# A two-branch attention kernel: its units ordered by a table of places, q and k in column halves, weight loads in halves on two queues, and warm-up matmuls on zeros

## The chip, the cores and the metric

The kernel runs on one core of one Trainium2 chip. A core has five engines with a queue each: PE (TensorE, matmuls; its weight loads are listed apart as PEld), ACT (ScalarE), DVE (VectorE), POOL (GpSimd) and SP (SyncE, which here only issues DMAs). They run side by side and wait for each other by semaphores. The metric is the device time of one execution in microseconds (us); less is better.

## The reference, cut to what matters

```python
def _A_ref(x, wqkv, w_phi, wo):                 # linear attention, H=32 heads of 20, S=2048, D=640
    q, k, v = ...                               # x @ wqkv, split into heads
    pq, pk = q @ w_phi, k @ w_phi               # per head
    phi_q = concat([softmax(pq), softmax(-pq)]) # phi_k likewise
    kv  = einsum('bhsf,bhsd->bhfd', phi_k, v)
    num = einsum('bhqf,bhfd->bhqd', phi_q, kv)
    den = einsum('bhqf,bhf->bhq', phi_q, phi_k.sum(s)) + 1e-06
    return (num / den) @ wo

def _B_ref(x, wq, wk, wv, wo, beta):            # 4 segments of 512 rows, memory M, z
    for s in range(4):
        a_dot = softmax(qs @ ks.T * scale + causal mask) @ vs
        a_mem = (phi(qs) @ M) / (phi(qs) @ z + 1e-06)   # phi(t) = t+1 if t>0 else exp(t)
        o_s = g * a_mem + (1 - g) * a_dot               # g = sigmoid(beta)
        M += phi(ks).T @ vs; z += phi(ks).sum()
    return concat(o_s) @ wo

g = sigmoid((x * gate_w).sum(-1))
out = g * _A_ref(x, ...) + (1 - g) * _B_ref(x, ...)
```

## The kernel before, in words

x has 2048 rows, worked on as 16 chunks of 128 rows, four chunks to a segment. It is needed with its columns on the partitions (xT): the first four chunks come in plainly (x_nat) and are transposed by PE (L435), the other twelve by transposing DMAs on SP (L363).

Branch B (local attention and memory), per segment: for each chunk the projections to k and q (b_kq, L518, through proj, L506: five matmuls of 128x320 per half of the columns, L510), a copy of each half out of its PSUM bank to kq (L462 on ACT or L464 on DVE), a store of kq to a DRAM buffer kd (L529), and the exponential and min/max of phi(k) (L536, L540, L543). When all four chunks are stored, transposing DMAs bring back groups of four heads as kqT (L864). Per pair of groups, five products of q and k go to the four PSUM banks called st (L893, four row tiles of 32 at once), each is read by one exponential over 2048 columns on ACT into one of six PT buffers (L899), POOL masks the diagonal (L905), and PE multiplies by v (L920, "pv"). There are 80 such products, 20 per segment, and one st, so a product waits until the exponential before it has read st. The memory term is L959 (am) with the update L986 (upd).

Branch A: projections of v and k (a1, L598; k's with folded weights), two exponentials (L609), sums, a reciprocal, a normalisation on POOL (L623), and the products kv (L644, L660). Then, per segment, the products pq (L735) with two exponentials (L743), den (L757), num (L796, read by DVE's ts, L802), and the final projections fin (L843), copied out and stored by chunk (L853).

All products but st share four PSUM banks w_76 to w_79. A bank is held from a group's first matmul until ACT or DVE has read it.

The order of the instructions on every engine is made by a Planner when the kernel is built. Each op has an engine (or two to choose from), an estimated duration, dependences, and a key. The planner walks a modelled time; when an engine is free it takes the ready op with the smallest key (after a flag, pri, that puts ops on a held bank first). Keys come from formulas whose numbers stand in PRM (L26), such as PRM["a0"] + PRM["a1"] * n for the n-th attention step (ak, L858). The engines then run these fixed orders; what waits blocks all behind it on its engine or its DMA queue. Two loads that matter at the start are beta_b (L352) and Wc (L350), small ones on SP; the large weights WkB, WqB, WvB, WvA and WqA are issued whole by ACT.

## Time and profile before

| | |
|---|---|
| median of 3 runs | 338.96 us (337.43 to 340.62) |
| profiled execution, its own time | 342.3 us |
| its span, first to last instruction | 340.6 us |
| PE busy | 306.5 us (90%) |
| ACT busy | 252.9 us (74%) |
| DVE busy | 231.4 us (68%) |
| POOL busy | 203.0 us (60%) |
| mean granted TensorE clock | 0.960 |

The profile is of one execution. Busy time of PE is modelled at the ends of matmuls, so a busy PE may still be slow, and the granted clock is a column of its own: 1.00 is 2.4 GHz, 0.50 is 1.2 GHz. A wait is put down to the engine whose work came last. Idle time matters on the engine that bounds the stretch.

### The profile page before, as it was taken

What the parts mean: (1) busy time and instruction counts of PE and PEld (TensorE: products, weight loads), DVE (VectorE), ACT (ScalarE), POOL (GpSimd) and SP (SyncE); (2) the same over time, 40 slices, a digit from 0 to 9 for tenths busy, and PEclk for the clock granted to TensorE, in tenths of its full rate; (3) what the DMA queues carried; (4) which work ended last, traced back from release to release, by engine and by line L of the source; (5) the groups of instructions that cost most, each with busy time, mean ns of one, the idle gap of its engine ahead of it and who ended that gap; (6) DMA issues with size and microseconds to landing.
All of it is one profiled execution on the core that took longest, in us unless ns stands there. A gap on an engine that the chain in (4) does not pass through costs nothing.

```text
span 340.6 us, 9847 instructions
## 1 busy us (share of the span) xinstructions
PE 306.5 (90%) x4002; PEld 211.0 (62%) x4002; DVE 231.4 (68%) x568; ACT 252.9 (74%) x330; POOL 203.0 (60%) x338
## 2 busy tenths in 40 slices
PE   2699988999899989989999898998999989968996
PEld 2377667666577765667655654665664755645774
DVE  3342686579867789999964877788773887596400
ACT  1367995788785799778899797985699788846342
POOL 8200197748557579497754486667764687588210
PEclk9999995899999999999899997999999999985999
DMA  7845936761012613022787383544488535312421
GB/s 266 295 187 129 137 70 73 159 139 64 2 64 79 163 26 113 14 92 36 251 153 118 141 149 75 142 62 138 101 155 185 96 96 129 80 22 66 120 67 58
DMA packets 78535, 38.42 MB, mean 113 GB/s; under 512 B 65818, under 2 KB 76442, under 8 KB 78490
## 3 DMA queue, kind: packets, MB, share of 16 engines
q1 hardware_dynamic: 75210, 33.70, 42.5%
q10 hardware_dynamic: 3280, 4.10, 3.4%
q8 instruction: 31, 0.51, 0.7%
q14 instruction: 14, 0.11, 0.1%
HBM read 6.42 MB, written 15.60 MB: 65 GB/s over the span
## 4 chain that ended last, share of the span: by engine, by line
PE 49%; DVE 20%; ACT 12%; POOL 9%; issue 5%; DMA 3%; SPq 0%; DVEq 0%; ACTq 0%
PE w_79 L510 6%; PE w_78 L510 6%; PE w_76 L510 5%; PE w_77 L510 5%; PE st_75 L893 4%; DMA beta_b<-in_B_beta_dram 3%; PE w_78 L843 3%; PE w_77 L843 3%; PE w_76 L920 3%; PE w_79 L843 2%; DVE ts_2711 L802 2%; PE w_76 L843 2%; ACT PT_122 L899 2%; ACT PT_121 L899 2%; DVE rm_127 L939 1%
## 5 line engine op out<-in xcount | busy, mean ns | idle before, releaser
L510 PEld LDWEIGHTS <-xT 128*128 128x128 bf16 x800 | 76.3, 100 | 46.3 <-issue 17.1
L899 ACT ACTIVATE PT_118<-st_75 128x2048 bf16<-128x2048 f32 x14 | 26.3, 1877 | 3.5 <-PE st_75 L893 3.5
L899 ACT ACTIVATE PT_117<-st_75 128x2048 bf16<-128x2048 f32 x14 | 26.4, 1883 | 2.9 <-PE st_75 L893 1.9
L899 ACT ACTIVATE PT_121<-st_75 128x2048 bf16<-128x2048 f32 x13 | 24.5, 1882 | 5.1 <-PE st_75 L893 5.0
L899 ACT ACTIVATE PT_122<-st_75 128x2048 bf16<-128x2048 f32 x13 | 24.5, 1882 | 5.0 <-PE st_75 L893 5.0
L899 ACT ACTIVATE PT_120<-st_75 128x2048 bf16<-128x2048 f32 x13 | 24.7, 1899 | 3.1 <-PE st_75 L893 3.1
L899 ACT ACTIVATE PT_119<-st_75 128x2048 bf16<-128x2048 f32 x13 | 24.6, 1895 | 3.1 <-PE st_75 L893 3.0
L905 POOL TENSOR_SCALAR_AFFINE_SELECT PT_117<-PT_117 128x512 bf16<-128x512 bf16 x22 | 14.2, 654 | 10.4 <-ACT PT_117 L899 10.4
L905 POOL TENSOR_SCALAR_AFFINE_SELECT PT_118<-PT_118 128x512 bf16<-128x512 bf16 x23 | 14.8, 656 | 7.1 <-ACT PT_118 L899 7.1
L905 POOL TENSOR_SCALAR_AFFINE_SELECT PT_122<-PT_122 128x512 bf16<-128x512 bf16 x21 | 13.4, 650 | 8.6 <-ACT PT_122 L899 8.6
L905 POOL TENSOR_SCALAR_AFFINE_SELECT PT_119<-PT_119 128x512 bf16<-128x512 bf16 x21 | 13.3, 644 | 6.7 <-ACT PT_119 L899 6.7
L905 POOL TENSOR_SCALAR_AFFINE_SELECT PT_120<-PT_120 128x512 bf16<-128x512 bf16 x20 | 12.9, 651 | 7.3 <-ACT PT_120 L899 7.3
L617 DVE TENSOR_REDUCE ksum_168<-Ek_160 128x32 f32<-128x640 bf16 x16 | 12.6, 813 | 6.4 <-ACT Ek_160 L609 6.4
L735 PEld LDWEIGHTS <-WqA 128*128 128x128 bf16 x100 | 9.4, 99 | 10.9 <-issue 2.5
L920 PEld LDWEIGHTS <-PT_118 128*128 128x128 bf16 x224 | 15.1, 96 | 1.7 <-issue 1.6
L905 POOL TENSOR_SCALAR_AFFINE_SELECT PT_121<-PT_121 128x512 bf16<-128x512 bf16 x21 | 13.7, 665 | 3.2 <-ACT PT_121 L899 3.1
L920 PEld LDWEIGHTS <-PT_117 128*128 128x128 bf16 x224 | 15.1, 96 | 0.5 <-issue 0.4
L617 DVE TENSOR_REDUCE ksum_169<-Ek_161 128x32 f32<-128x640 bf16 x16 | 12.5, 814 | 4.2 <-ACT Ek_161 L609 4.1
L920 PEld LDWEIGHTS <-PT_122 128*128 128x128 bf16 x208 | 14.1, 96 | 1.3 <-issue 1.2
L578 POOL TENSOR_TENSOR Cd_139<-omgS,omg_b 128x128 f32<-128x128 f32 x2 | 0.8, 399 | 22.6 <-DVE omgS L572 22.4
L920 PEld LDWEIGHTS <-PT_121 128*128 128x128 bf16 x208 | 13.7, 96 | 0.8 <-issue 0.4
L920 PEld LDWEIGHTS <-PT_119 128*128 128x128 bf16 x208 | 14.1, 97 | 0.1
(658 smaller groups left out, 1100.0 us busy)
## 6 DMA issues: line engine op xcount, KB each, us to landing
kd_60<-kq_95 SPq DMA_DIRECT2D x2, 512.0 KB, 2.6
kd_61<-kq_96 SPq DMA_DIRECT2D x2, 512.0 KB, 3.3
kd_62<-kq_97 SPq DMA_DIRECT2D x2, 512.0 KB, 2.8
kd_63<-kq_95 SPq DMA_DIRECT2D x2, 512.0 KB, 3.4
out_dram<-osb_2724 SPq DMA_DIRECT2D x6, 160.0 KB, 1.9
WkB<-in_B_wk_dram ACTq DMA_DIRECT2D x1, 800.0 KB, 5.3
WqB<-in_B_wq_dram ACTq DMA_DIRECT2D x1, 800.0 KB, 8.1
WvB<-in_B_wv_dram ACTq DMA_DIRECT2D x1, 800.0 KB, 11.5
```

The lines of the kernel that those rows point to most:

```text
L510: nc.tensor.matmul(w[:, 0:width], lhsT=T["xT"][:, c, sc * P:(sc + 1) * P], rhs=T[Wn][:, c, 320 * hf:320 * hf + width], start=(c == 0), sto ...
L578: nc.gpsimd.tensor_tensor(out=T[dst][s % 2], in0=og[:, :, None].to_broadcast([P, 4, H]), in1=T[src][:, None, :].to_broadcast([P, 4, H]), o ...
L617: op("DVE", 0.74, lambda sgn=sgn: nc.vector.tensor_reduce(out=T["ksum"][js][:, H * sgn:H * sgn + H], in_=T["Ek"][ik][:, sgn].rearrange("p ...
L735: nc.tensor.matmul(w, lhsT=T["WqA"][:, c, t * P:(t + 1) * P], rhs=T["xT"][:, c, s * L:(s + 1) * L], start=(c == 0), stop=(c == KC - 1))
L802: op("DVE", dve_t(320), lambda w, sgn=sgn: nc.vector.tensor_tensor(out=T["ts"][d][:, sgn], in0=w[:, 0:320].rearrange("p (h d) -> p h d", d ...
L843: nc.tensor.matmul(w[:, 0:320], lhsT=T[nm][j][:, k5, :], rhs=T[Wo][:, k5, hf * 320:hf * 320 + 320], start=(i == 0), stop=(i == 9))
L893: nc.tensor.matmul(st4[:, i, o:o + w], lhsT=T["kqT"][j][r:r + 32, 0, c * P:(c + 1) * P], rhs=T["kqT"][j][r:r + 32, 1, c * P:L], start=True ...
L899: op("ACT", act_t(2048), lambda: nc.scalar.activation(out=T["PT"][slot], in_=st4, func=ACT.Exp, scale=SCALE_B), r=("st4",), w=(("PT", slot ...
L905: nc.gpsimd.affine_select(out=v, in_=v, pattern=[[0, 4], [1, P]], compare_op=ALU.is_ge, fill=0.0, base=0, channel_multiplier=-1)
L920: nc.tensor.matmul(w[:, j * 84 + i * V1:j * 84 + (i + 1) * V1], lhsT=T["PT"][slot][:, i, o + (j - c) * P:o + (j - c + 1) * P], rhs=T["vB"] ...
L939: nc.vector.tensor_tensor(out=rd, in0=rd, in1=T[C][s % 2][:, :, 4 * g:4 * g + 4], op=ALU.mult)
```

## The change

**Order.** PRM goes. A table of 441 numbers gives a key to each unit of work: one projection with its copy, one step of attention, one group of kv, and so on. The keys of ops in one unit are equal. The formulas stay only as defaults. The planner's estimates change too (shorter hops to the next engine, shorter pv and st products, one DMA line for both queues with at most eight transfers under way), ops that only later members of a bank's group need are made to hold back the group's first op, and non-attention groups no longer need two free banks to begin.

**q and k in halves.** b_kq works on one half of the columns of one chunk: two projections, two copies, a store of 128x1024, phi(k) of 320 columns. kq is half as wide and has six buffers. Transposes of heads of one half wait only for the four stores of that half. phik's halves and the exponentials' buffers are kept apart.

**Loads.** WkB, WqB and WvB come in halves of 320 columns, some on ACT's queue and some on SP's. WvA and WqA move to SP, behind the first stores. sig_b's exponential gets a later key.

**Start.** DVE zeroes a tile, ACT runs one exponential on it, PE runs NWARM = 12 matmuls of 128x512 on it. All four copies of xT are DVE's.

**End.** The output of a chunk is stored in two halves.

```diff
-PRM = {"a0": -9.65, "a1": 0.97, "v0": 2.4, "v1": 2.28, "i1": 3.91, "d1": 3.58, "i2": 24.29,
...
+TABLE = (32379, -8395, -7202, -45515, -9326, -21479, -14085, -40063, -5810, 810, -5549, -11546,
...
-    HOP = {"PE": 0.27, "ACT": 0.20, "DVE": 0.18, "POOL": 0.13, "SP": 0.1, "X": 0.0}
+    HOP = {"PE": 0.20, "ACT": 0.18, "DVE": 0.18, "POOL": 0.12, "SP": 0.1, "X": 0.0}
...
+    def unit(self, default):
+
+        n = len(self.keys)
+        self.keys.append(self.table[n] / 100 if n < len(self.table) else default)
+        return Unit(n)
...
+        for lst in banks.values():
+            head, busy = lst[0], sum(o.dur[0] for o in lst if "PE" in o.eng)
+            for o in lst[1:]:
+                for p in o.preds:
+                    if p.bank is not head.bank and p not in head.preds:
+                        head.preds[p] = 0.0 if "PE" in o.eng else busy
...
-                        need = 1 if o.att else 2
-                        if n < need:
+                        if not n:
                             continue
-                        st = max(st, sorted(free)[need - 1])
+                        st = max(st, min(free))
+                    if o.q is not None:
+                        st = max(st, lands[0])
...
-    dma(wload("WkB", B_wk, q="ACT"), (), ("WkB",), -1998, 819, eng="ACT")
-    dma(wload("WqB", B_wq, q="ACT"), (), ("WqB",), -1997, 819, eng="ACT")
...
+    xload(0)
+    wpart("WkB", B_wk, 0, -1998)
+    xload(2)
+    wpart("WqB", B_wq, 0, -1997)
+    wpart("WkB", B_wk, 1, -1996, eng="SP")
+    wpart("WqB", B_wq, 1, -1995)
+    wpart("WvB", B_wv, 0, -1994, "WvBw", eng="SP")
+    wpart("WvB", B_wv, 1, -1993, "WvBw")
...
+    dma(wload("WvA", A_wqkv[:, 2 * D:3 * D]), (), ("WvA",), -10, 819, release=15.0)
+    dma(wload("WqA", A_wqkv[:, D:2 * D]), (), ("WqA",), -9, 819, release=18.0)
...
+    op("DVE", 0.13, lambda: nc.vector.memset(T["PT"][0][:, 0], 0.0), w=(("PT", 0),), key=-4000)
...
+    op("ACT", 1.4, lambda: nc.scalar.activation(out=T["rd"][0][:, 0], in_=T["PT"][0][:, 0, 0:4],
+                                                func=ACT.Exp), r=(("PT", 0),), w=(("rd", 0),), key=-1996.5)
+    for i in range(NWARM):
+        op("PE", 0.43 if i < 8 else 0.22, lambda: nc.tensor.matmul(
+            st4[:, 0, :], lhsT=T["PT"][0][:, 0, 0:P], rhs=T["PT"][0][:, 0, :], start=True,
+            stop=True), r=(("PT", 0),), w=("st4",), key=1e6)
...
-        op(("DVE", "ACT"), (0.7, 0.6), cp, w=(("xT", sc),), free=bk)
+        op("DVE", 0.42, lambda w, cp=cp: cp("DVE", w), w=(("xT", sc),), free=bk, key=-1000)
...
-    def b_kq(s, c, key):
-        i = (4 * s + c) % NKQ
+    def b_kq(s, c, hf, key):
+
+        i = (8 * s + 4 * hf + c) % NKQ
...
-            hv + (("kq", i),), (("kd", s, c),), key, 524)
+            (("kq", i, 0), ("kq", i, 1), ("kq", i)), (("kd", s, c, hf),), key, 262)
...
-                                                     scale=-1.0), r=("beta_b",), w=("sig",))
+                                                     scale=-1.0), r=("beta_b",), w=("sig",), key=-15)
...
-        ch = 4 * s + qc
-        dma(lambda: nc.sync.dma_start(out=out2[ch * P:(ch + 1) * P, :], in_=T["osb"][n]),
-            (("osb", n, 0), ("osb", n, 1)), (("out", ch),), key, 164)
+            rows = slice((4 * s + qc) * P, (4 * s + qc + 1) * P)
+            dma(lambda hf=hf, rows=rows: nc.sync.dma_start(
+                out=out2[rows, hf * 320:hf * 320 + 320],
+                in_=T["osb"][n][:, hf * 320:hf * 320 + 320]),
+                (("osb", n, hf),), (("out", s, qc, hf),), key, 82)
...
-            tuple(("kd", s, c) for c in range(4)), (("kqT", j),), key, 262, tr=True)
+            tuple(("kd", s, c, g // 4) for c in range(4)), (("kqT", j),), key, 262, tr=True)
```

The order itself at three places. First the beginning of DVE's row before the change: xT are the copies of the transposed chunks, WphiD needs Wc and sig_b needs beta_b.

```order
L377 CAST ident_b<-ident_f 128x128
L446 COPY xT<-w_77 128x5x128
L421 TENSOR_TENSOR WphiD<-Wc,m_92 128x140
L404 CAST ind<-bd_93 128x4
...
L421 TENSOR_TENSOR WphiD<-Wc,m_92 128x160
L446 COPY xT<-w_79 128x5x128
L454 COPY WvB<-w_76 128x5
...
L589 TENSOR_SCALAR sig_b<-sig_b 128x32
```

And the same place of the changed kernel, to the first gate column of WvB.

```order
L447 MEMSET PT_121 128x256
L448 CAST ident_b<-ident_f 128x128
L481 CAST ind<-bd_93 128x4
L523 COPY xT<-w_76 128x5x128
L523 COPY xT<-w_77 128x5x128
L617 TENSOR_SCALAR phik_101<-kq_95 128x16x20
L541 CAST kq_96<-w_79 128x4x4x20
L620 TENSOR_TENSOR phik_101<-phik_101,ek_107 128x16x20
L523 COPY xT<-w_76 128x5x128
L523 COPY xT<-w_77 128x5x128
L531 COPY WvB<-w_77 128x5
```

Four copies of xT instead of two stand on DVE, and all of them ahead of the first WphiD; the other two were ACT's, one of them behind sig_b.

Second, the end of the start on SP, before the change: kd are the stores of q and k, kqT the transposes that need all of the segment's stores.

```order
L348 DMA gw_row<-in_gate_w_dram 5x128
L350 DMA Wc<-in_A_w_phi_dram 128x5x20
L352 DMA beta_b<-in_B_beta_dram 128x32
L529 DMA kd_60<-kq_95 128x2048
L529 DMA kd_60<-kq_96 128x2048
L529 DMA kd_60<-kq_97 128x2048
...
L864 DMA_TRANSPOSE kqT_108<-kd_60 128x2x512
L363 DMA_TRANSPOSE xT<-in_A_x_dram 128x5x128
L864 DMA_TRANSPOSE kqT_109<-kd_60 128x2x512
```

And now:

```order
L396 DMA WkB<-in_B_wk_dram 128x5x320
L396 DMA WvB<-in_B_wv_dram 128x5x320
L419 DMA gw_row<-in_gate_w_dram 5x128
L421 DMA Wc<-in_A_w_phi_dram 128x5x20
L425 DMA beta_b<-in_B_beta_dram 128x32
L606 DMA kd_60<-kq_95 128x1024
L606 DMA kd_60<-kq_98 128x1024
L396 DMA WvA<-in_A_wqkv_dram 128x5x640
L606 DMA kd_60<-kq_97 128x1024
L606 DMA kd_60<-kq_96 128x1024
L396 DMA WqA<-in_A_wqkv_dram 128x5x640
L950 DMA_TRANSPOSE kqT_112<-kd_60 128x2x512
```

Two weight halves stand among the first loads, the four stores ahead of the first transpose are half as wide, and the two large weights of branch A stand between them.

Third, the end of ACT's row before the change, at the last eight of the 80 exponentials (PT); dz and osb are copies out of w banks.

```order
L899 ACTIVATE PT_117<-st_75 128x2048
L899 ACTIVATE PT_118<-st_75 128x2048
L462 COPY dz_2703<-w_76 128x128
L899 ACTIVATE PT_119<-st_75 128x2048
L899 ACTIVATE PT_120<-st_75 128x2048
L899 ACTIVATE PT_121<-st_75 128x2048
L899 ACTIVATE PT_122<-st_75 128x2048
...
L462 CAST osb_2724<-w_78 128x320
```

And now, from the 74th to the 78th:

```order
L985 ACTIVATE PT_122<-st_75 128x2048
L824 ACTIVATE Eq_3407<-w_79 128x512 x2
L985 ACTIVATE PT_123<-st_75 128x2048
L539 CAST osb_3437<-w_76 128x320
L985 ACTIVATE PT_124<-st_75 128x2048
L539 COPY dz_3413<-w_76 128x128
L985 ACTIVATE PT_125<-st_75 128x2048
L539 COPY dz_3414<-w_78 128x128
L985 ACTIVATE PT_126<-st_75 128x2048
L539 CAST osb_3436<-w_77 128x320
```

Exponentials that stood back to back now have another operation of ACT between them.

## Rows read from the trace of the kernel before

**Rows 1.** The page: the span, and busy time of each engine.
```profile
span 340.6 us, 9847 instructions
PE 306.5 (90%) x4002; PEld 211.0 (62%) x4002; DVE 231.4 (68%) x568; ACT 252.9 (74%) x330; POOL 203.0 (60%) x338
```
**Rows 2.** Stretches: us, busy PE, PEld, DVE, ACT, POOL; granted clock, DMA share, GB/s.
```profile
0.00:17.30 17.30, 8.05 (x41) 5.04 (x42) 5.41 (x14) 3.96 (x7) 9.20 (x33) 1.00 0.83 277
17.30:51.70 34.40, 32.41 (x320) 23.12 (x319) 19.05 (x43) 29.17 (x54) 10.91 (x11) 1.00 0.60 133
51.70:61.70 10.00, 9.73 (x137) 7.25 (x137) 5.12 (x11) 6.10 (x5) 7.55 (x16) 0.50 0.52 74
61.70:160.80 99.10, 92.95 (x1306) 67.04 (x1305) 83.78 (x173) 78.01 (x113) 67.74 (x105) 1.00 0.31 79
160.80:164.10 3.30, 3.30 (x27) 1.88 (x25) 3.30 (x7) 2.97 (x4) 2.95 (x7) 0.51 0.09 14
164.10:205.00 40.90, 38.08 (x519) 24.28 (x518) 29.95 (x89) 36.35 (x46) 23.54 (x41) 1.00 0.74 169
205.00:208.30 3.30, 3.07 (x12) 0.94 (x11) 1.77 (x5) 1.51 (x3) 2.64 (x4) 0.50 0.59 129
208.30:304.00 95.70, 87.19 (x1299) 58.56 (x1296) 71.24 (x198) 79.41 (x81) 65.23 (x107) 1.00 0.49 109
304.00:314.10 10.10, 8.44 (x97) 5.53 (x97) 7.08 (x19) 5.63 (x3) 9.12 (x14) 0.50 0.15 50
314.10:340.60 26.50, 23.26 (x258) 17.37 (x256) 4.67 (x14) 9.79 (x18) 4.17 (x6) 1.00 0.29 82
```
**Rows 3.** Timeline of PE, 0 to 20 us: start, us, operation, [idle before <-releaser].
```profile
4.36 0.72 PE L435 MATMUL w_76<-ident_b,x_nat 128*128 128x128 bf16 x5 [4.36 <-DMA x_nat<-in_A_x_dram]
...
9.28 1.52 PE L510 MATMUL w_77<-WkB,xT 128*128 128x320 bf16 x5
13.36 1.49 PE L510 MATMUL w_78<-WkB,xT 128*128 128x320 bf16 x5 [2.56 <-ACT xT L444]
...
17.30 0.84 PE L510 MATMUL w_77<-WqB,xT 128*128 128x320 bf16 x5
17.98 0.84 PE L510 MATMUL w_78<-WqB,xT 128*128 128x320 bf16 x5
```
**Rows 4.** Timeline of ACT at the start.
```profile
12.50 0.23 ACT L585 ACTIVATE sig_b<-beta_b 128x32 f32<-128x32 bf16 x1 [3.36 <-DMA beta_b<-in_B_beta_dram]
12.63 0.67 ACT L444 COPY xT<-w_78 128x640 bf16<-128x640 bf16 x1
```
**Rows 5.** Timeline of DVE at the start.
```profile
1.42 2.15 DVE L377 CAST ident_b<-ident_f 128x128 bf16<-128x128 f32 x1 [1.42 <-POOL ident_f L373]
...
10.47 0.30 DVE L421 TENSOR_TENSOR WphiD<-Wc,m_92 128x140 bf16<-128x140 bf16 x1 [4.34 <-DMA Wc<-in_A_w_phi_dram]
```
**Rows 6.** DMA issues: what, queue, count, KB each, us from issue to landing.
```profile
kd_60<-kq_95 SPq DMA_DIRECT2D x2, 512.0 KB, 2.6
...
WkB<-in_B_wk_dram ACTq DMA_DIRECT2D x1, 800.0 KB, 5.3
WqB<-in_B_wq_dram ACTq DMA_DIRECT2D x1, 800.0 KB, 8.1
...
x_nat<-in_A_x_dram SPq DMA_DIRECT2D x2, 320.0 KB, 4.9
...
kqT_108<-kd_60 SPq DMA_TRANSPOSE x2, 3.5
```
**Rows 7.** PE waits: who waited for L899; PE's timeline; PE's waits by total.
```profile
  PE st_75 L893: 3.9, 8
...
51.93 0.61 PE L893 MATMUL st_75<-kqT_110 32*128 32x512 bf16 x4 [1.42 <-ACT PT_121 L899]
...
PE w_76 L920 <- DVE ts_2711 L802: 1.6, 2, 1.3
```
**Rows 8.** Timeline of ACT, 300 to 312 us.
```profile
306.59 1.88 ACT L899 ACTIVATE PT_121<-st_75 128x2048 bf16<-128x2048 f32 x1 [3.90 <-PE st_75 L893]
```
**Rows 9.** Groups of ACT: busy us, mean ns | idle before.
```profile
L536 ACT ACTIVATE ek_104<-kq_95 128x640 bf16<-128x640 bf16 x2 | 1.5, 734 | 0.0
```

More of the change, by code (lines that the diff above doesn't have):

```diff
@@ L113, in plan @@
         order = []
+        banks = {}
+        for o in self.ops:
+            if o.bank is not None:
+                banks.setdefault(o.bank, []).append(o)
+        for lst in banks.values():
[4 more added lines that the diff above has]
+                        head.preds[p] = 0.0 if "PE" in o.eng else busy
         for o in self.ops:
             o.npred = len(o.preds)
-            for p in o.preds:
-                p.succs.append(o)
+            for p, slack in o.preds.items():
+                p.succs.append((o, slack))
         for o in self.ops:
@@ L165, in plan @@
                 lat, qd = o.q
-                qav[e] = max(qav[e], o.end + lat) + qd
-                land = qav[e] + 0.4
+                qav = max(qav, o.end + lat) + qd
+                land = qav + 0.5
+                lands = lands[1:] + [land]
             if o.free is not None:
@@ L359, in wt_load @@
             (), ("WT",), key, 819, tr=True, release=rel)
-    dma(wload("WqA", A_wqkv[:, D:2 * D], q="ACT"), (), ("WqA",), -1992, 819, eng="ACT")
     for sc in range(4, NCH):
@@ new lines, in b_v @@
+        wd = 320 + hf
+        k = U(key)
+        bk = proj(4 * s + c, "WvB", (("WvBw", hf),) + (("WvBg",) if hf else ()), hf, k, wd)
+        cv = copy_to(lambda w: (T["vB"][b][:, c, hf * 16:hf * 16 + 16, 0:DH],
+                                w[:, 0:320].rearrange("p (h d) -> p h d", d=DH)))
+        if hf == 0:
+            op(AD, cp_t(320), cv, w=(("vB", b, c, hf),), free=bk, key=k)
+        else:
+            op(AD, cp_t(320), cv, w=(("vB", b, c, hf),), r=(bk,), key=k, use=bk)
+            op("DVE", 0.07, lambda w: nc.vector.tensor_copy(
+                out=T["gl"][:, 4 * s + c:4 * s + c + 1], in_=w[:, 320:321]),
+               w=(("gl", s, c),), free=bk, key=k)
@@ L749, in a3_den @@
         bk = bank()
+        key = U(key)
         first = True
@@ L1072 @@
     b_upd = untagged(b_upd_)
-    A1K = [-9, -8, -7, -6] + [PRM["v0"] + PRM["v1"] * c for c in range(NCH - 4)]
+    A1K = [-9, -8, -7, -6] + [2.4 + 2.28 * c for c in range(NCH - 4)]
     def a1_four(p):
@@ L1089 @@
         b_upd(0, q, 12 + q)
-    seg_in(1, [PRM["i1"] + PRM["d1"] * c for c in range(4)])
+    seg_in(1, 3, 1)
     a1_four(1)
@@ L1096 @@
     a1_four(2)
-    seg_in(2, [PRM["i2"] + PRM["d2"] * c for c in range(4)])
+    seg_in(2, 23, 1)
     a1_four(3)
```

200 lines of the change are left out of this document (99 added, 101 removed), and 35 rows, old and new, of the table TABLE.

## The prediction

> **What bounds the kernel now.** I read the page's busy shares first: PE is busy for 306.5 of 340.6 us, ACT for 253, DVE for 231 [rows 1]. PE is the engine to follow, and time can come from three places only: PE idle, PE at half clock, and the work itself, which the change leaves alone apart from twelve warm-up matmuls. Second I cut the span where the granted clock changes [rows 2]; the reader is to see ten stretches. After the start, the clock is half in four of them, 10.0 + 3.3 + 3.3 + 10.1 = 26.7 us long, with PE busy for 9.73 + 3.30 + 3.07 + 8.44 = 24.5 us of it. Span less PE busy, over the nine stretches from 17.3 on, is 2.0 + 0.3 + 6.2 + 0 + 2.8 + 0.2 + 8.5 + 1.7 + 3.2 = 24.9 us. The last 3.2 us are nearly all the end, the last copy and store after the last matmul, so 21.7 us are stalls. The first 17.3 us hold another 9.2 us of idle.
>
> Third, the timeline of PE at the start [rows 3]: the first projection starts at 9.28, the second only at 13.36, 2.56 us of that waiting for a copy of xT on ACT; the three groups from 13.36 to 17.30 take 1.31 us each, the next one 0.68 (17.30 to 17.98). So the clock is half up to about 17.3, though the column of granted clocks says 1.00 there: five matmuls of 320 columns in 1.31 us are the 1.2 GHz level, in 0.68 us the 2.4 GHz level. What held the copy up is in the timeline of ACT [rows 4]: sig_b stood ahead of it and waited 3.36 us for the small load of beta_b. DVE did the same with Wc, 4.34 us [rows 5]. The loads of that time land by bytes, in the order of issue [rows 6]: x's first pair of chunks and WkB (1120 KB) are in at 0.81 + 5.3 = 6.1 us, with x's second pair and WqB (2240 KB) at 1.33 + 8.1 = 9.4 us, some 340 KB per us between.
>
> Fourth, who PE waits for in the middle: the st bank, when ACT's exponential has not read it (3.9 us in 8 waits, one of 1.42 us at 50.5, just ahead of the half-clock stretch at 51.7), and banks that DVE has not emptied, ts first [rows 7]. Near the end the two feed each other: ACT sits idle for 3.90 us until PE's next st product lets it go on at 306.59 [rows 8], inside the second long half-clock stretch.
>
> **The start.** The change puts all four xT copies on DVE, ahead of everything that needs Wc or beta_b. It loads the first projection's operands (x's first pair and half of WkB, 720 KB) first and, with x's second pair and half of WqB, 1440 KB by 6.1 + 320/340 = 7.0 us. PE first runs 12 matmuls of 128x512 on zeros. From 1.31 us for 5 x 320 columns such a one costs 0.42 us at half clock and from 0.68 us it costs 0.22, so all twelve 2.6 to 5.0 us. DVE's first operation stands at 1.42 [rows 5]; its memset, which waits for nothing, can be done at about 1.2, so PE is in the warm-ups until 3.8 to 6.2 us. I take 6.2, since the trace shows half clock until long after work began. The real transposes, which could start at 4.36 [rows 3], are then late by 1.9 us, and the clock is full. From there: two transposes to 6.8, copies to 7.4, K to 8.1, Q to 8.8 (its weights are in at 7.0), two more transposes to 9.4, copies hidden behind one projection, and the fourth projection ends at about 10.9. Before, four are done at 17.30. That is **-6.4 us**. If zeros raise no clock, four projections at 1.31 us end at about 13.3: -4. If the warm-ups end at 4.4, -8. The third and fourth weight halves and WvB are needed from the seventh projection on, at about 12.5 us. They make 2640 KB, in at 9.4 + 400/340 = 10.6.
>
> WvA and WqA go to SP behind stores of q and k. WvA is queued behind the stores of the sixth projection and first read by the nineteenth, some twelve groups of 0.68 us later, so 8 us; an 800 KB load took 5.3 and 8.1 us from issue in company [rows 6]. That is just in time; I price it at nothing, and at 1 us if it is late. WqA has four groups more.
>
> **Halves of q and k.** The matmuls are the same 800 projections. Twelve exponentials of 640 columns at 0.74 us [rows 9] become 24 of 320. With the whole 0.74 us as a bound for each extra piece, ACT gets 0 to 8.9 us more, on an engine that is idle for 88 us; the DVE pieces likewise. Cover: PE's work between a projection and its next reader. If that cover were gone I would pay it once, within the stalls below. SP issues 16 more stores and 16 more output parts at a few tenths of a us each, spread over the run. The first half's stores now come before the second half's projections, so the transposes that feed the first attention products have more PE work ahead of them. A store takes 2.6 us and a transpose 3.5 [rows 6], about 7 us with the issue. In the changed order I count at least some 12 us of PE work between the last projection of each half and the first product that reads it, and over 20 in all seven later halves. So nothing is late there; nothing is gained either, as PE did not wait there before.
>
> **The order.** In the old order the products that feed ACT are uneven: thirty-one groups of PE work between the 20th and the 21st, then pairs at the end with ACT's exponentials back to back, where one takes 1.88 us [rows 8] and PE has less than that to do. In the new order no two products have more than eight groups between them, and near the end ACT has another operation between nearly all exponentials. The nums, whose DVE ts held the banks, are spread between them too. How much of the 21.7 us goes? At least nothing (the stalls move), at most three quarters, 16 us: DVE and ACT stay at over 68% and four banks are still four. The st waits (3.9 us) should nearly vanish and bank waits shrink where nums spread out; I take half, **-10.8 us**.
>
> **The clock.** 24.5 us of PE work at half clock would take 12.3 at full, if PE is what matters there. The stretches begin just after stalls: one at 51.7 after 1.42 us [rows 7], one at 304 after a stretch in which PE was short of work. Fewer stalls, fewer stretches: 0 to -12.3, and half again, **-6.1 us**.
>
> The Trainium skill's page "TensorE: Matmul & The Clock Gate", section "Why this matters for your kernels", speaks against this term: it asks for much longer idle gaps than the 1.42 us here before the clock falls. By it the term would be nothing and the sum 6.1 us higher. This trace disagrees with its row at 51.7, so I keep the term and give the rule a rival.
>
> **The sum.** 340.6 - 6.4 - 10.8 - 6.1 = 317.3 us of span. The profiled execution took 342.3 us, 1.7 more than its span, and the median of the three timed runs is 338.96, 3.3 less. So 317.3 + 1.7 - 3.3 = 315.7; I say 316.
>
> **The rivals.**
> A, forecast: 316; 0.58.
> B, the new order does nearly all it can: -8 - 16 - 12.3, span 304.3, time 303. For it: no dependence that I counted is tight. Against: 68 to 74% on two other engines [rows 1]. 0.15.
> C, only the start changes, and stalls and half-clock stretches reappear elsewhere, so the table doesn't do what it says: 340.6 - 6.4 - 1.6 = 332.6, or 335 with -4. For it: the banks, the single st and the loads on DVE and ACT are what they were. Against: the even spacing. 0.17.
> D, the start and the stalls as in A, while the clock stays half for as long as before: 321.8. Against it is the stretch at 51.7. 0.05. It is the page's rule above, as a result.
> E, slower: SP is served in order, and 32 stores instead of 16, each waiting for two copies, stand ahead of transposes. One handoff that is late costs store and transpose again, 6.1 us [rows 6], plus PE at half clock behind it, some 1.6 us (half of 3.3). Three of the eight late, 23.1 us, eat the 23.3 us of gain; with four the time is 316 + 31 = 347. Against it: 12 to 20 us of PE work per handoff. 0.05.
>
> **Range and chances.** B gives the low end, 303. C with a small start gives 335; 333 leaves out less than half of C and E, together with a little below 303 some 0.15. So 303 to 333. A's own range is 309 to 324. A measurement here tells about 1% (3.4 us) from no change, so faster is below 335.6: all of A, B, D, and most of C: 0.90. Same, 335.6 to 342.3: the rest of C, 0.05. Slower: E, 0.05.
>
> **What would show it.** Right: the first projection at 7 to 8 us at 0.68 us per five, four done by 11; no wait of ACT on beta_b; PE idle after the start near 14 us; at most two half-clock stretches. The start is wrong if projections still take 1.31 us after the warm-ups. The order is wrong if PE still idles for over 18 us, or has as many half-clock stretches. If kqT transposes are waited for by PE, it is E.

## The result, and the profile after

The changed kernel takes 320.25 us (median of 4 runs, 319.93 to 321.6) against 338.75 us for the kernel before on the same chip: a ratio of 0.946 (95% interval 0.940 to 0.951). The forecast was 316 us in a range of 303 to 333. The profiled execution took 320.51 us. Ratios and intervals here leave out executions more than 1.5% above the fastest of the same kernel.

The page after answers to [rows 1]:

```profile
span 318.8 us, 9982 instructions
PE 294.4 (92%) x4005; PEld 204.5 (64%) x4014; DVE 245.8 (77%) x601; ACT 250.5 (79%) x335; POOL 202.6 (64%) x341
```

PE's busy time falls by 12.1 us, though its matmuls are the same plus twelve warm-ups (4014 weight loads in place of 4002; nine records of matmuls are missing from this trace). DVE's rises by 14.4 us. The second of these will matter.

The stretches, against [rows 2], cut where four projections are done (columns as there):

```profile
0.00:11.57 11.57, 8.98 (x52) 4.73 (x53) 5.92 (x10) 2.81 (x5) 9.43 (x36) 1.00 0.91 272
11.57:318.80 307.23, 285.37 (x3955) 199.77 (x3961) 239.84 (x591) 247.68 (x330) 193.14 (x305) 1.00 0.49 115
```

No half-clock stretch is left after the start. From the end of the start on, PE is busy for 285.4 us where it was busy for 306.5 - 8.05 = 298.4, that is -13.0; its idle time there is 307.23 - 285.37 = 21.9 us where it was 24.9, that is -3.0. The start takes 11.57 us in place of 17.30, -5.7. Together that is -21.7, the span's way from 340.6 to 318.8 within rounding.

PE's timeline at the start, against [rows 3]:

```profile
7.99 0.85 PE L587 MATMUL w_78<-WkB,xT 128*128 128x320 bf16 x5 [1.20 <-DVE xT L523]
8.68 0.84 PE L587 MATMUL w_79<-WqB,xT 128*128 128x320 bf16 x5
...
10.88 0.85 PE L587 MATMUL w_79<-WqB,xT 128*128 128x320 bf16 x5
11.57 0.84 PE L587 MATMUL w_76<-WqB,xT 128*128 128x320 bf16 x5
```

The first projection starts at 7.99 us and each takes 0.69 to the next: full clock from the first one. The second has no wait for its weights. But PE waited 1.20 us for the copy of xT on DVE. The timelines of DVE and then of POOL for that moment, against [rows 5]:

```profile
6.42 1.48 DVE L481 CAST ind<-bd_93 128x4 bf16<-128x4 f32 x1 [2.73 <-POOL bd_93 L477]
6.54 1.36 DVE L523 COPY xT<-w_76 128x640 bf16<-128x640 bf16 x1
6.95 0.96 DVE L523 COPY xT<-w_77 128x640 bf16<-128x640 bf16 x1
```
```profile
6.34 0.66 POOL L487 MEMSET vB_110<- 128x128 bf16 x1
6.58 0.98 POOL L487 MEMSET vB_111<- 128x128 bf16 x1
7.15 0.73 POOL L484 MEMSET phik_101<- 128x384 bf16 x1
```

The third and fourth copies of the same shape take 0.48 us. The first two stand behind a cast of only four columns, which itself shows 1.48 us while POOL fills buffers. This is the first sign of what took the place of the old stalls.

What PE waits for, in total and longest, against [rows 7]:

```profile
PE w_78 L724 <- DVE tm_136 L1030: 2.1, 1, 2.1
PE w_77 L587 <- DVE vA_161 L541: 1.4, 1, 1.4
...
PE st_75 L979 <- ACT PT_123 L985: 0.4, 1, 0.4
```

The waits on the st bank are down from 3.9 us in eight to 0.4 us in one. Every large wait after the start is now for DVE. One of them, read backwards, in three timelines (PE, DVE, POOL):

```profile
168.54 0.70 PE L587 MATMUL w_77<-WkB,xT 128*128 128x320 bf16 x4 [1.38 <-DVE vA_161 L541]
```
```profile
165.66 0.17 DVE L1025 TENSOR_TENSOR rd_129<-rd_129,Cd_144 128x16 f32<-128x16 f32 x1
...
166.03 2.05 DVE L1025 TENSOR_TENSOR rm_131<-rm_131,Cm_146 128x16 f32<-128x16 f32 x1
168.00 0.48 DVE L541 CAST vA_161<-w_77 128x320 bf16<-128x320 f32 x1
```
```profile
165.68 2.37 POOL L702 TENSOR_TENSOR EkN_169<-Ek_165,krec_175 128x1280 bf16<-128x1280 bf16 x1 [0.58 <-DVE rd_129 L1024]
```

Two multiplications of 128x16, the same instruction: 0.17 us, and 2.05 us when it starts just after POOL's EkN (165.68 to 168.05) and ends with it. The bank of PE's next product is emptied only then. The 56 small multiplications rd and rm take 28.6 us here, where they took 20.4 before; if all were as short as the shortest (0.174 us) they would take 9.7. DVE's busy time in these instructions alone, now (L1025) and before (L939):

```profile
0.00:318.80 318.80, 28.64 (x56) 1.00 0.50 121
```
```profile
0.00:340.60 340.60, 20.41 (x56) 0.96 0.47 113
```

In the changed kernel 32 of the 56 take over 0.25 us, and each of these ends 0.02 to 0.04 us after the end of an instruction of POOL: 12 after a mask of PT, 10 after oA, 8 after EkN, two after others. Of the 24 short ones only one runs wholly beside a POOL instruction. The eight behind EkN make up 10.2 of the 18.9 us above the shortest. Before, 18 took over 0.25 us, three of them behind EkN with 4.8 us.

### The profile page after: what moved, and what is told of

It reads as the page before. It is cut to its first block, busy times and chain, and to the rows that moved or that the text cites. A ratio compares the mean times of both kernels' runs of the same rounds, so it can differ in the third digit from the quotient of the medians.

```text
span 318.8 us, 9982 instructions
## 1 busy us (share of the span) xinstructions
PE 294.4 (92%) x4005; PEld 204.5 (64%) x4014; DVE 245.8 (77%) x601; ACT 250.5 (79%) x335; POOL 202.6 (64%) x341
## 4 chain that ended last, share of the span: by engine, by line
PE 45%; DVE 30%; POOL 10%; issue 6%; ACT 6%; DMA 2%; POOLq 0%; SPq 0%; DVEq 0%; ACTq 0%
PE w_78 L587 5%; PE w_77 L587 5%; PE w_79 L587 4%; PE st_75 L979 4%; PE w_76 L587 4%; PE w_78 L927 3%; DMA WvA<-in_A_wqkv_dram 2%; PE w_79 L927 2%; PE w_77 L1006 2%; DVE rm_131 L1025 2%; DVE ts_3422 L885 2%; PE w_77 L927 2%; DVE ksum_173 L696 2%; PE w_79 L816 2%; DVE ts_3423 L885 2%
## 5 line engine op out<-in xcount | busy, mean ns | idle before, releaser
L587 PEld LDWEIGHTS <-xT 128*128 128x128 bf16 x800 | 74.2, 97 | 43.6 <-issue 15.4
L991 POOL TENSOR_SCALAR_AFFINE_SELECT PT_121<-PT_121 128x512 bf16<-128x512 bf16 x22 | 14.1, 649 | 12.8 <-ACT PT_121 L985 12.8
L991 POOL TENSOR_SCALAR_AFFINE_SELECT PT_122<-PT_122 128x512 bf16<-128x512 bf16 x23 | 15.1, 667 | 7.7 <-ACT PT_122 L985 7.7
L991 POOL TENSOR_SCALAR_AFFINE_SELECT PT_124<-PT_124 128x512 bf16<-128x512 bf16 x20 | 13.1, 664 | 7.9 <-ACT PT_124 L985 7.9
L991 POOL TENSOR_SCALAR_AFFINE_SELECT PT_126<-PT_126 128x512 bf16<-128x512 bf16 x21 | 13.7, 663 | 5.9 <-ACT PT_126 L985 5.9
L991 POOL TENSOR_SCALAR_AFFINE_SELECT PT_123<-PT_123 128x512 bf16<-128x512 bf16 x21 | 13.3, 642 | 6.4 <-ACT PT_123 L985 6.4
L991 POOL TENSOR_SCALAR_AFFINE_SELECT PT_125<-PT_125 128x512 bf16<-128x512 bf16 x21 | 14.1, 684 | 5.2 <-ACT PT_125 L985 5.1
L1006 PEld LDWEIGHTS <-PT_122 128*128 128x128 bf16 x224 | 15.1, 96 | 0.7 <-issue 0.5
L1006 PEld LDWEIGHTS <-PT_121 128*128 128x128 bf16 x224 | 15.1, 96 | 0.4
L1006 PEld LDWEIGHTS <-PT_123 128*128 128x128 bf16 x208 | 14.0, 96 | 1.2 <-POOL PT_123 L991 0.7
L1006 PEld LDWEIGHTS <-PT_126 128*128 128x128 bf16 x208 | 13.8, 96 | 0.6 <-POOL PT_122 L991 0.2
L1006 PEld LDWEIGHTS <-PT_124 128*128 128x128 bf16 x208 | 13.8, 96 | 0.4 <-issue 0.2
L1006 PEld LDWEIGHTS <-PT_125 128*128 128x128 bf16 x208 | 13.8, 96 | 0.4
```

The lines of the kernel that those rows point to most:

```text
L587: nc.tensor.matmul(w[:, 0:width], lhsT=T["xT"][:, c, sc * P:(sc + 1) * P], rhs=T[Wn][:, c, 320 * hf:320 * hf + width], start=(c == 0), sto ...
L991: nc.gpsimd.affine_select(out=v, in_=v, pattern=[[0, 4], [1, P]], compare_op=ALU.is_ge, fill=0.0, base=0, channel_multiplier=-1)
L1006: nc.tensor.matmul(w[:, j * 84 + i * V1:j * 84 + (i + 1) * V1], lhsT=T["PT"][slot][:, i, o + (j - c) * P:o + (j - c + 1) * P], rhs=T["vB"] ...
```

## The experiments

The lock theory, called L below: a DVE instruction that has two operands in SBUF (or is a copy, cast or scalar operation from SBUF to SBUF) is held while a POOL instruction runs, until that one ends. The Trainium skill states such a lock on its page "SBUF — State Buffer", section "Who interferes with whom": one of the two holds a shared port for its whole instruction. The rows above agree, with 2.05 against 0.17 us. The rivals were that DVE is merely loaded, that it is a share of the port that POOL takes, and that the halves or the table cost DVE its time in other ways.

**Reciprocals in PSUM.** In the changed kernel the reciprocal goes to spare columns of the bank, so the multiplication has one operand in SBUF; instruction for instruction the order is the same.

```diff
-nc.vector.reciprocal(out=rd, in_=x[:, :, :, DH])
-nc.vector.tensor_tensor(out=rd, in0=rd, in1=T[C]..., op=ALU.mult)
+rp = w[:, 336:352].rearrange("p (j i) -> p j i", i=4)
+nc.vector.reciprocal(out=rp, in_=x[:, :, :, DH])
+nc.vector.tensor_tensor(out=rd, in0=rp, in1=T[C]..., op=ALU.mult)
```

> The changed kernel; only the small reciprocals of the attention's normalisation (rd, rm) write into unused columns of their PSUM bank, so that the multiplication after them reads one operand from SBUF instead of two. The order of all engines is unchanged. Theory L (these multiplications are held up while POOL normalises EkN, since both want the same way into SBUF; the PE stalls behind DVE come from that): rd and rm, which now take up to 2.05 us and 28.7 us in sum, all take under 0.3 us; PE idle after the start falls from 18.6 us (21.9 less 3.3 of tail) to 8 to 13; time 310 to 316. Rival N (DVE is merely busy, 246 of 319 us, and late for that): rd and rm keep their long ones or the waits go to the next operation; time 319 to 321.

Measured: 314.93 us (310.95 to 315.54), ratio to before 0.926 (0.920 to 0.933), 5 us better than the change alone. DVE's groups in this run (shape, count, busy us, mean ns, idle before):

```profile
L1026 DVE TENSOR_TENSOR rd<-w,Cd 128x16 f32<-128x16 f32 x32 | 5.6, 175 | 1.2
L1026 DVE TENSOR_TENSOR rm<-w,Cm 128x16 f32<-128x16 f32 x24 | 4.2, 175 | 0.9
```

28.6 us have become 9.8, every one at 0.17 to 0.18, though 33 of the 56 run wholly beside an instruction of POOL. L holds for these: it is the second operand in SBUF that gets them held. DVE's busy time falls by only 10.0 us (245.8 to 235.8), since other instructions are held longer now: the 24 scalar operations on phiq take 17.0 us in place of 11.8. The traced run gained its time in spite of a worse start: there the cast of ind was held for 3.89 us, the first projection started at 10.47, and the clock fell again behind the long wait (the second projection takes 1.33 us to the next operation):

```profile
10.47 1.07 PE L587 MATMUL w<-WkB,xT 128*128 128x320 bf16 x5 [4.48 <-DVE xT L523]
11.34 1.54 PE L587 MATMUL w<-WqB,xT 128*128 128x320 bf16 x5
```

So the start, too, varies with where POOL's fills meet the cast. The same was in the trace of the kernel without the table, below.

The same edit in the kernel before:

> The kernel before with the same edit (reciprocals of rd and rm into PSUM). Theory L: rd and rm are 20.3 us there, 10.8 above their shortest; two PE stalls (0.52 at 69.4, 1.00 at 135.4) and some more stand behind them, so 2 to 6 us come off 338.75: 333 to 337; less than in the changed kernel, as its order puts fewer of them beside EkN. Rival N: 338 to 340.

Measured: 335.27 us, ratio 0.988 (0.985 to 0.992), a gain of 3.8 us against 5.3 in the changed kernel. The lock was there before the change, and was worth somewhat less. The two traces with this edit also compare the two orders with rd and rm free in both. From the fifth projection on, the kernel before and then the changed one:

```profile
16.50:332.80 316.30, 292.22 (x3963) 203.84 (x3960) 219.39 (x554) 248.46 (x323) 194.32 (x305) 0.98 0.45 106
```
```profile
15.42:313.00 297.58, 284.30 (x3964) 199.13 (x3961) 229.04 (x591) 247.21 (x330) 193.31 (x305) 1.00 0.48 119
```

PE idles 24.1 us in the old order and 13.3 in the new. Without the edit it was 24.9 and 21.9: in these traces freeing rd and rm takes 0.8 us of PE's idle time in the old order and 8.6 in the new. Part of the old order's gain is clock instead (0.960 against 0.979 in the two traces).

**EkN in pieces.** The other side of the lock: POOL's multiplication in four pieces of 128x320; rd and rm as in the changed kernel.

```diff
-nc.gpsimd.tensor_tensor(out=EkN, in0=Ek, in1=krec, op=ALU.mult)     # 128x1280
+for h in range(0, 2 * H, 16):
+    nc.gpsimd.tensor_tensor(out=EkN[:, h:h+16], in0=Ek[:, h:h+16], in1=krec[:, h:h+16], op=ALU.mult)
```

> The changed kernel with GpSimd's EkN multiplication (128x1280, 2.36 us, 16 of them) issued in four pieces of 128x320; all else in the same order, DVE's small multiplications rd and rm still with two operands in SBUF. Theory L (DVE's instruction is held until the GpSimd instruction that runs beside it ends): the longest rd or rm falls from 2.05 to about 0.7 us, their sum from 28.7 to under 24 us, the stalls of PE behind them go as with the reciprocals in PSUM, 314 to 317 us. Theory P (the two engines share a port, and what DVE loses is GpSimd's total traffic): the longest may fall, the sum of DVE's busy time stays at 244 to 247 us, 319 to 321. Rival C: 48 more instructions on GpSimd, each some 0.1 us more, delay the KV matmuls that wait for EkN: 321 to 324.

Measured: 315.79 us (315.19 to 316.23), ratio 0.934 (0.931 to 0.937).

```profile
L1029 DVE TENSOR_TENSOR rd<-rd,Cd 128x16 f32<-128x16 f32 x32 | 13.0, 406 | 1.2
L1029 DVE TENSOR_TENSOR rm<-rm,Cm 128x16 f32<-128x16 f32 x24 | 8.8, 365 | 0.9
```

21.8 us in place of 28.6, the longest single one 0.84 us in place of 2.05; DVE busy 236.0. (Behind a piece of EkN none takes over 0.65 us; the one of 0.84 stands behind oB, which the edit leaves whole.) A hold until the POOL instruction ends gives this; by theory P, in which DVE loses in proportion to POOL's whole traffic, DVE would have stayed at 244 to 247. After a start as in the changed kernel, its stretch from 11.57 to the end holds 15.3 us of PE idle, against 21.9 in the changed kernel:

```profile
11.57:313.80 302.23, 286.96 (x3964) 201.46 (x3961) 230.07 (x591) 246.99 (x330) 200.27 (x353) 0.99 0.49 117
```

**Without the table.** The changed kernel with `TABLE = ()`, so that the units have the default keys, and all else of the change.

> The changed kernel with an empty table: every unit takes the default formula's place, all other parts (halves, loads, warm-ups, the planner's new estimates) stay. Theory T (the table carries the gain behind the start): half-clock stretches and st waits come back, 328 to 340. Rival P (the planner's better estimates and the start carry it): 319 to 325, clock over 0.99.

Measured: ratio 0.979 (0.974 to 0.984), some 332 us, against 0.946 with the table (all five executions 331.53 to 338.06; the traced one took 337.18). In its trace rd and rm take 20.1 us:

```profile
L990 DVE TENSOR_TENSOR rm<-rm,Cm 128x16 f32<-128x16 f32 x24 | 10.4, 433 | 0.9
L990 DVE TENSOR_TENSOR rd<-rd,Cd 128x16 f32<-128x16 f32 x32 | 9.7, 303 | 1.2
```

So without the table some 12 of the 18.5 us of gain are gone (theory T). Not all of that need be the table's: in this trace the cast of ind was held for 3.89 us, and the fifth projection starts at 15.35 in place of 11.57; whether the other executions share that start is not known. It is also the table, not the halves, that brings rd and rm beside EkN more often: eight times with it, four without, three before (28.6, 20.1 and 20.4 us). The mean granted clock of the runs compared was 0.964 to 0.969, in the changed kernel 0.993 to 1.0: without the table the half-clock stretches come back. PE's idle time from the fifth projection on is 22.6 us in this trace, against 21.9 with the table: nothing here shows the table to save stalls while rd and rm are held. No run takes the halves of q and k or the planner's new estimates back by themselves; their own worth is not shown.

**Small loads out of the way, alone.** In the kernel before, sig_b and WphiD are issued behind the four copies of xT, by a reordering of the planner's list after it is made:

```diff
+late = [t for t in self.order if t[1].late]          # sig_b, WphiD
+last = max(i for i, t in enumerate(self.order) if t[1].early)      # copies of xT
+self.order = (those up to last that are not late) + (the late ones) + (the rest)
```

> The kernel before; only sig_b on ACT and WphiD on DVE are issued after the four copies of xT, all else in the old order. Theory S (the wait for beta_b and Wc is worth its 2.56 us of PE idle at the start): the second projection starts by 10.9 instead of 13.36, 2 to 4 us less: 334.5 to 337. Rival H (the time is taken back by WqB, in at 9.4, or by half clock): 338 to 339.5.

Measured: 336.6 us, ratio 0.993 (0.990 to 0.996), -2.5 us, theory S. In its trace the fifth projection starts at 14.14 in place of 17.30. The rest of the start's -5.7 us is left to the halves of the loads and the warm-ups, which the next two runs take away.

**No warm-ups.** The changed kernel without the matmuls of zeros. (There are twelve; the expectation's "sixteen" is a slip.)

> The changed kernel without its sixteen warming matmuls of zeros (nothing that is read depends on them), everything else in the same order. Theory W (the warm-ups give the projections the full clock): in the changed kernel five matmuls of a projection took 0.68 us from the start; before, without warm-ups, 1.31. Here the first four or five projections take 1.31 again, +0.63 each, +2.5 to +3.2 us, less what the transposes gain because PE is free before 6.2 us (x_nat is there at about 4.4, so up to -1.5): 320.5 to 323. Theory N (warm-ups only take PE's time; the start is set by the copies of xT on DVE): 318 to 320.

Measured: 323.23 us (322.68 to 324.0), 3.0 us worse than the change. PE's timeline:

```profile
4.45 1.25 PE L510 MATMUL w<-ident_b,x_nat 128*128 128x128 bf16 x10 [4.45 <-DMA x_nat<-in_A_x_dram]
7.97 1.51 PE L585 MATMUL w<-WkB,xT 128*128 128x320 bf16 x5 [2.27 <-DVE xT L521]
9.27 1.54 PE L585 MATMUL w<-WqB,xT 128*128 128x320 bf16 x5
```

The transposes start 1.6 us earlier and nothing comes of it: the first projection starts at 7.97 in place of 7.99, since DVE is held to the same moment. Then the first projection takes 1.30 us to the next, and the fifth starts at 13.93 in place of 11.57. Theory W: with the matmuls of zeros the projections run at full clock from the first, without them they do not.

**Whole weight loads.** The changed kernel with WkB, WqB and WvB whole on ACT's queue.

```diff
-    fn = wload(dst, src[:, lo:hi], lo, hi, q=eng)
+    last = ((w or dst) == "WvBw") == (hf == 1)
+    fn = wload(dst, src[:, 0:D], 0, D, q="ACT") if last else None
```

> The changed kernel with WkB, WqB and WvB loaded whole (800 KB each), all three on ACT's queue, as in the kernel before; order otherwise unchanged, warm-ups and halves of q and k as changed. By bytes in order of issue x's first pair and WkB, 1120 KB, were in at 6.1 us before and WqB at 9.4 to 9.6: theory H (halves let the second projection start): the first projection starts as now (7 to 8 us), the second at 9.5 instead of 8.68, four done 0.8 to 1 us later than at 11.57: 320.5 to 322. Theory N (the copies of xT on DVE set the start, not the weights): four done by 11.9, 319.5 to 320.7. If the half-idle PE loses the clock again at the start: 322 to 324.

Measured: 321.96 us (320.57 to 322.95), ratio 0.950 (0.942 to 0.958).

```profile
9.60 0.84 PE L588 MATMUL w<-WqB,xT 128*128 128x320 bf16 x5 [0.78 <-DMA WqB<-in_B_wq_dram]
```

The second projection waits for WqB until 9.60, as theory H says to a tenth, in place of 8.68. That the halves are worth that 0.9 us at the start is shown. The difference of the medians, 1.7 us, lies within the spread of the two, and the traced execution ends only 0.1 us later (span 318.9) than the changed kernel's.

**POOL's fills later.** Held back until the second copy of xT, by a copy of one column of xT ahead of them on POOL:

```diff
+nc.gpsimd.tensor_copy(out=ident_f[:, 0:1], in_=xT[:, 0, 2 * P - 1:2 * P])      # then the nine fills
```

> The changed kernel with GpSimd's nine fills (padding of phik, ones of vB, Msb) held back until the second copy of xT is done (a one-column copy of xT on GpSimd goes ahead of them); all else in the same order. Theory L (a fast copy of DVE from PSUM to SBUF is held as long as GpSimd runs its fills): the first two copies of xT take 0.5 us each instead of 1.36 and 0.96 (3.8 in other profiles of kernels with the same start), the cast of ind 0.1 instead of 1.5, the first projection starts at 7.0 to 7.3 us instead of 7.99 (10.5 in the others), and the median falls by 0.8 to 3 us to 317 to 319.5. Theory X (the copies are slow for another reason, as the transposes that still come in): copies as before, 320 to 321. If the fills that come later hold what follows (phik_101, vB), the gain is given back by 14 us: 320 to 322.

Measured: 319.46 us (319.33 to 320.99), ratio 0.946 (0.942 to 0.949): not to be told from the change. DVE's timeline says why:

```profile
6.40 0.17 DVE L489 CAST ind<-bd 128x4 bf16<-128x4 f32 x1 [2.71 <-POOL bd L485]
...
8.37 2.08 DVE L629 TENSOR_SCALAR phik<-kq 128x320 bf16<-128x320 bf16 x1 [1.01 <-ACT kq L551]
```

The cast of ind falls from 1.48 to 0.17 us, and the first projection starts at 7.02. It was the cast that was held, not the copies (they read PSUM) as I had written in the expectation. But the fills now run when the max-and-add on phik_101 is due, which is held for 2.08 us (0.47 in the changed kernel, 0.25 with the fills later still, below), with the third and fourth copies behind it: the case named last in the expectation.

**The three edits together, and the fills later still.** Reciprocals in PSUM, EkN in pieces, fills behind the second copy of xT; then the same with the fills behind the fourth.

> The changed kernel with the three edits together: reciprocals of rd and rm in PSUM, GpSimd's fills after the second copy of xT, EkN in four pieces. If the losses to the lock of DVE and GpSimd add up: 314.9 with the first edit alone, less 1 to 3 us at the start, less 1 to 3 us for the multiplications of phiq that EkN still holds (excess of 16 us in the first edit's profile, little of it ahead of PE): 309 to 313. If DVE is no longer what PE waits for after the first edit: 313 to 315.

> The kernel with the three edits together, with GpSimd's fills held back until the fourth copy of xT (instead of the second) and the fill of Msb behind the first gates. Theory L: in the run with the fills after the second copy the max-and-add on phik_101 was held 2.08 us (8.37 to 10.45) beside them and the third and fourth copy of xT came only at 11.0; here it takes 0.25 us, the copies come at about 9.5, the four projections are done at 10.8 to 11.2 instead of 13.1: 312.0 less 1.5 to 2.2 = 309.8 to 310.5. Rival: WvB's halves, which land at about 10.5 to 12.7, or other work of DVE hold the next projections, and PE waits there instead: 311 to 312.5.

Measured: 312.01 us (311.75 to 312.81), ratio 0.923 (0.920 to 0.927); and 310.41 us (310.08 to 310.62), ratio 0.915 (0.909 to 0.921), the fastest version of the study; both are within what was expected of the lock. The page of the second, and PE's largest wait by total:

```profile
span 308.6 us, 10048 instructions
PE 294.2 (95%) x4005; PEld 204.7 (66%) x4014; DVE 226.6 (73%) x601; ACT 249.1 (81%) x335; POOL 209.3 (68%) x390
```
```profile
PE w L1025 <- POOL PT L1010: 3.0, 4, 0.9
```

Against the changed kernel's profile the span is 10.2 us shorter and PE's busy time 0.2: what went is idle time of PE, 24.4 to 14.4 us. DVE is no longer the one waited for longest.

**Stalls put in.** The clock was the other open point: the changed kernel has stalls of up to 2.07 us (PE's L724 at 157.67, behind tm_136) with the granted clock at 1.00 all through, and the kernel before lost it at a stall of 1.42 us. DVE repeats one normalisation at three places.

```diff
-nc.vector.tensor_tensor(out=out_ap(), in0=x[...], in1=T["r" + nm]..., op=ALU.mult)
+for _ in range(1 + ({6: 6, 16: 12, 24: 20}.get(n, 0) if nm == "d" else 0)):
+    nc.vector.tensor_tensor(out=out_ap(), in0=x[...], in1=T["r" + nm]..., op=ALU.mult)
```

> The changed kernel with three stalls put in: DVE repeats one normalisation of a bank (128x320, writes the same values again) 6, 12 and 20 times more, at about 83, 185 and 251 us of the changed kernel's timeline, so that the bank is late by some 2.6, 5 and 8.5 us; order unchanged. PE has 1 to 2 us of other work each time. Theory K (a stall makes the clock fall, the longer the surer): the granted clock, 1.00 in all of the changed kernel, shows a half-clock stretch of 3 to 10 us behind the second and the third stall, perhaps the first; time 320 + 12 of stalls + 2 to 5 for each stretch, 335 to 345. Theory O (the clock does not follow stalls of this length; it fell before for another reason, such as what ran on the other engines): clock stays 1.00, time 320 + 10 to 14 = 330 to 334.

Measured: 342.27 us (341.58 to 344.54), 22 us more than the change. PE's timeline at the three places, and the stretches of and behind the first and the third stall:

```profile
95.86 0.46 PE L573 MATMUL w<-WphiD,WT 128*128 128x140 bf16 x3 [3.20 <-DVE oB L1031]
...
196.09 0.44 PE L1046 MATMUL w<-Mbd,phiq 128*128 128x84 bf16 x4 [4.23 <-DVE td L1031]
...
272.77 1.49 PE L927 MATMUL w<-WoA,oTA 128*128 128x320 bf16 x5 [8.82 <-DVE td L1031]
```
```profile
92.60:95.80 3.20, 0.06 (x1) 0.00 (x0) 3.00 (x8) 1.63 (x1) 1.22 (x2) 0.96 0.87 115
95.80:98.50 2.70, 2.64 (x23) 2.63 (x23) 2.05 (x7) 0.99 (x2) 0.00 (x0) 0.50 0.04 8
...
263.90:272.70 8.80, 0.04 (x4) 0.07 (x1) 8.26 (x18) 3.77 (x6) 0.00 (x0) 0.63 0.17 39
272.70:276.30 3.60, 3.53 (x43) 2.34 (x43) 2.09 (x5) 0.00 (x0) 2.81 (x4) 0.50 0.00 0
```

All three took the clock with them, 3.20 us as well as 8.82 (theory K). Span +21.0: PE idle +15.4 (24.4 to 39.8) and PE busy +5.6 (294.4 to 300.0). As far as PE's busy time shows it, the clock costs a third of what the stalls do.

**One stall filled.** Is the stall at 50.5 in the kernel before the cause of the half-clock stretch from 51.7 to 61.7, and what is that stretch worth? 28 matmuls of 128x92 go into it, to columns that nobody reads.

```diff
+if (p, bi, c) == (0, 5, 1):
+    for _ in range(28):
+        nc.tensor.matmul(w[:, 420:512], lhsT=EkN[:, 0:P], rhs=vA[:, 0:92], start=False, stop=True)
```

> The kernel before with 28 matmuls of 128x92 put into one stall of PE, the one of 1.42 us at 50.5 (they go to columns of a bank that nobody reads; order otherwise unchanged). Theory K (that stall is what brings the half-clock stretch from 51.7 to 61.7): the stall is filled, the stretch is gone, PE's 9.73 us of work in it take about 4.9, and 4 to 5 us are gained if the clock keeps up afterwards: 334 to 335.5 against 339. Theory M (the clock falls there for what goes on around it, not for this stall): the stretch is still there, 338.5 to 340. Theory G (the gain is given back: PE, faster there, waits for ACT's exponentials or loses the clock in a later stall): the stretch is gone or moves, 336.5 to 338.5.

Measured: 339.51 us (12 runs) against 340.37 (17 runs), ratio 0.997 (0.994 to 1.001). Two of its stretches, and one matmul of PE behind the filled place:

```profile
52.00:54.00 2.00, 1.08 (x21) 0.78 (x18) 0.37 (x2) 1.63 (x1) 2.00 (x2) 1.00 0.69 119
...
58.00:60.00 2.00, 2.00 (x17) 1.44 (x15) 1.13 (x3) 1.74 (x1) 1.45 (x8) 1.00 0.45 105
```
```profile
53.68 0.40 PE L898 MATMUL st<-kqT 32*128 32x384 bf16 x8 [0.92 <-ACT PT L904]
```

The clock stays at 1.00 where it was 0.50, so PE's idle time there was the cause (not M). The kernel before with reciprocals in PSUM, which keeps this stall (1.43 us at 51.13), shows half clock behind it again. By the time alone, 0.9 us below the kernel before, M would not be out; the trace decides. PE, now fast, waits for ACT's exponentials (0.92 us there). The same four exponentials in both traces, first the kernel before, then this one, give the worth:

```profile
49.96 1.91 ACT L899 ACTIVATE PT_121<-st_75 128x2048 bf16<-128x2048 f32 x1
...
64.18 1.91 ACT L899 ACTIVATE PT_119<-st_75 128x2048 bf16<-128x2048 f32 x1
```
```profile
49.35 1.91 ACT L904 ACTIVATE PT<-st 128x2048 bf16<-128x2048 f32 x1
...
61.41 1.91 ACT L904 ACTIVATE PT<-st 128x2048 bf16<-128x2048 f32 x1
```

This run was 0.61 us ahead at the first pair and 2.77 us at the second: the stretch was worth 2.2 us, where half of PE's 9.73 us of work in it is 4.9. All exponentials up to 158 us stay 2.77 us ahead. So G, with its mechanism seen; the gain in the medians, 0.9 us, is not told from zero.

## Why the prediction was right, and where its working was not

The time and the sign were right, and the sum close: -21.7 us of span measured, -23.3 predicted. Two of its three terms were not. In time the miss is larger, 320.25 against 316, and 3.0 of these 4.3 us come from one step: the sum took 3.3 us off because the execution profiled before lay that far above its median. The execution profiled after lies only 0.3 us above its own. What had made the one before slow was most likely its half clock, which the clock term already gave back.

**The start: -5.7 for -6.4.** The mechanism is right step by step: no wait for beta_b, projections at full clock, first one at 7.99. Four were done at 11.57 in place of the 10.9 of the sum. The step that failed is "copies to 7.4": DVE, behind the cast of ind that POOL's fills held, had them done at 7.9. I had read that the copies take 0.5 us and not asked what stands ahead of them. The slower cast of ident_b in [rows 5], 2.15 us, was most likely the same thing in plain sight: it took 0.77 us in the run with reciprocals in PSUM. Taken away alone the warm-ups cost 3.0 us and the halves of the loads 0.9 at the start; the small loads, moved alone in the kernel before, gave 2.5. WvA, whose lateness was priced at nothing, made PE wait 0.4 us.

**The stalls: -3.0 for -10.8.** This term failed. What I said of the order came true as far as it went: the st waits fell from 3.9 to 0.4 us. The failed step is that the bank waits "shrink where nums spread out", since I took DVE's lateness to come from uneven work. A good part of it came from single instructions held beside POOL, and the new order lets more of them meet EkN (28.6 us of rd and rm in place of 20.4). With the lock eased by EkN in pieces, PE idles 15.3 us after the start, close to the 14 that I had asked for; with all three edits

```profile
11.23:308.60 297.37, 284.98 (x3952) 199.77 (x3959) 221.32 (x591) 246.17 (x330) 203.52 (x363) 0.99 0.50 119
```

it is 297.37 - 284.98 = 12.4. So the new order is good for that term, and the lock took most of it back. The comparison with rd and rm free in both orders says the same: 24.1 us of idle time in the old, 13.3 in the new, -10.8. The sign by which I would have called the order wrong (over 18 us idle) showed up, while the other (many half-clock stretches) did not: they were not two signs of one thing.

**The clock: -13.0 for -6.1.** I halved it for want of a better bound; all of it came. Two things make it less of a gain than it looks. The profiled execution of before had a mean clock of 0.960, the same kernel's timed runs among the experiments mostly 0.975 to 0.98. By the loss of clock (0.040 against 0.020 to 0.025), an estimate, some 5 to 6.5 of the 13.0 us were not in the median. And PE at half clock hides waits that PE at full clock shows: filling the stall was worth 2.2 us of the 4.9. Stalls and clock are therefore no separate terms. Their sum, -16.0 against -16.9 predicted, was about right because the error of one was the error of the other with its sign turned. That is luck and not a sum that held. How much of the 7.8 us of missing stall gain is that exchange and how much the lock, no run divides exactly, since the clock differs between the runs compared.

**The rivals.** C, only the start: the kernel without the table comes to it (some 332 us), so what is left without the table is C's time, and the table does do what it says. D, the clock stays as it was: it did not. E, late handoffs: no wait of PE for kqT among its larger waits. B, nearly all: with the lock eased the kernel is at 310, B's 303 is not reached.

**The rule on the clock.** In the changed kernel a stall of 2.07 us did not take the clock and, with delays put in, one of 3.20 did. The rule on idle gaps of the Trainium skill's page "TensorE: Matmul & The Clock Gate", section "Why this matters for your kernels", would have both so. In the kernel before a stall of 1.42 us did take the clock, and with that one stall filled it stayed, which the rule would not have. Nor does the length of a stall by itself decide it: with the small loads moved, the same wait of 1.42 us (at 48.76) left the clock at 1.00, and it fell at the next one, of 0.92 us (at 51.13). Shortly before the stall of 2.07 us and the one of 1.42, PE ran products of 21 columns; what tells them apart stays open.

## What to carry to other kernels

Before pricing a stall by the load of the engine that is waited for, look at the shortest and the longest duration of each of its small instructions; where one shape takes 0.17 us here and 2.05 us there, look at what POOL does at that moment, and move an operand to PSUM or cut POOL's long instruction before touching the order. Don't add up stalls and half clock as if each were worth its full time: price them as one term, from the stretch, with the next engine's pace as its limit. And in a start, ask of every copy what stands ahead of it on its queue, and what other engine runs beside that.
